# A residual block as nested fast convolution: row blocks, row sums and second-layer weights laid out anew, with a new order of all instructions

## The chip, the cores and the metric

The kernel runs on one core of one Trainium2 chip. The metric is the device time of one execution in microseconds (us). The kernel before took 462.77 us as the median of three runs (462.04 to 462.83).

## The reference

The input x has 2 images of 512 channels and 64 x 64 points in bf16. Group normalisation goes over 4 groups of 128 channels.

```python
def reference(x, t_emb, g1, be1, w1, w_emb, g2, be2, w2):
    ...
    def conv3(z, w):
        zp = jnp.pad(z, ((0, 0), (0, 0), (1, 1), (1, 1)))
        taps = [jnp.einsum("bchw,oc->bohw", zp[:, :, i:i+H, j:j+W], w[:, :, i, j]) for i in range(3) for j in range(3)]
        ...
    h = conv3(_silu(gn(x, g1, be1)), w1)
    emb = _silu(t_emb) @ w_emb
    h = h + emb.reshape(B, C, 1, 1)
    h = conv3(_silu(gn(h, g2, be2)), w2)
    return x + h
```

Two 3 x 3 convolutions from 512 to 512 channels carry nearly all the work.

## The kernel before

**Fast convolution.** The rows of an image are taken in groups of four (row r belongs to kind r modulo 4). From four kinds of rows and two halo rows, the kernel makes six *row planes* by sums, differences and scalings (`vplane`, s = 0 to 5). Each plane is multiplied by its own combination of the three weight rows, and the six results are combined into four output rows again. That saves matrix products and costs elementwise work. In most of the kernel the planes 0 to 3 are transformed once more along the columns (the "A" and "B" groups of matmuls with 256 columns), and in the last chunk the two outer planes 4 and 5 too (the "C" and "D" groups).

**Chunks and units.** A chunk `c` is a layer, an image and half of the rows: eight chunks, 0 to 3 for the first convolution and 4 to 7 for the second. A chunk has four input-channel tiles `ct` of 128 channels and four output-channel tiles `k`. The *unit* `u{c}{k}` makes one output tile: it runs the matmuls of TensorE (PE) into PSUM, the copies out of PSUM on ScalarE (ACT; `evac_o`, `evac_m`, `evac_pair`, `evac_b`), and VectorE's (DVE's) sums: "A", "s" and "d" on the four row results M, scalings by 8, 2 and 4, and "y" for the four output rows. `OO` holds the two outer results, which are added to two of the output rows ("O" on DVE, or "oa", an accumulating DMA of GpSimd's queue).

**Row blocks.** For each chunk and input tile, `load_a` brings the rows of a half image into a buffer of 18 strips (one strip, RP = 130 elements, is a row of a kind; four strips are a kind, PL = 520; `FO` orders the kinds). Before, the two halo strips are the first and the last one. `silu` works on it in place. `rows_a` and `rows_b` then make the planes: `k` is 4 times the block, then instructions of two kinds at a time, each written `two(base, r0, r1)`: two pieces of 520 elements, r1 − r0 apart. In the variant `early`, which only chunk 0 uses, the planes 4 and 5 are complete at the end of `rows_a`; otherwise their second term is added at the end of `rows_b` (by DVE, or with `vacc` by an accumulating DMA).

**Weights.** First-layer weights are combined on the core (`prep_w1`, `nest_w1`). Second-layer weights are combined by `prep_w2(j, ct)`, one output tile and one input tile at a time: two loads, two scalings on ACT, sums on DVE, one store to `u_scr` in HBM; two raw buffers are used in turn. `fetch_w2(j)` reads four of them back and adds the column combinations for the first chunk of layer 2; `stream_w2` takes later ones from HBM.

**Output.** The first layer's result goes to `h_scr` in HBM with its sums for the second normalisation. In layer 2 the output tensor is filled with x first (copies "pre" from HBM to HBM), and units accumulate into it by DMA; the last unit adds x on DVE.

**One tile, one order.** All buffers are slices of one large SBUF tile, `ar`. The semaphore waits between instructions are derived by the framework from the accesses to that tile, and it compares the block from an access's first to its last element. Each instruction is an operation of the class `Plan` with a number. `Plan.op` collects its predecessors element by element, and `emit` issues all operations, some 2,790, in the order of a long string `ORDER`, two characters per operation. Each engine executes its own in that order; SyncE's (SP's) queue issues the plain DMAs, GpSimd's (POOL's) the accumulating ones. `after` and `seq` are extra predecessors given by hand: `after` keeps a prefill copy behind the start of a unit four units earlier, `seq` keeps the first loads in sequence.

**Lines.** Small helpers record operations, so many instructions share a line: `tt` (L345, a DVE instruction with two tensor inputs), `ts` (L349, a DVE scaling), `act` (L368), `dma` (L383), `memz` (L387) and `mm` (L398). L1119 is the batch statistics of x's first tile.

Of the kernel before, what the change touches and what calls it, by code (L numbers as in the profile page):

```python
# [26 lines left out]
class Plan:  # L27
# [19 lines left out]
    def op(self, eng, cost, fn, r=(), w=(), name="", chain=False, lat=None, slack=0.0, after=None, sw=False, seq=None):  # L47
# [68 lines left out]
def _idx(off, dims):  # L116
# [6 lines left out]
FO = (3, 1, 2, 0)  # L123
# [3 lines left out]
AF = 18 * RP  # L127
VP = 4160
# [25 lines left out]
    'w2d': ((0, 0, 0, 0), (0, 0, 0, 0), (3, 3, 3, 3), (4, 0, 0, 0), (0, 0, 0, 0), (0, 0, 0, 0), (0, 0, 0, 0), (0, 0, 0, 0)),  # L154
# [14 lines left out]
    "0N002g0P0O0M0l010Q020304050607080k0R1G0j1D0a0i1E0g0p0b0h1F0m0o0n0c0q1I1H1J0r0s0d0t1K0u1L0T1M2Z1N0v0w240U0x0y2W0e0f1O130V"  # L169
    "1Y1i3P1P0X1Q1R1j0z1k160S210_1l3X1m2B0-1S2C1b0W1n2p090A0B0C0D0E0F2E0G0H0I0J0K0L1o102D1p1T111q2F2G1r4v191s3R2H1U122h2I1t2J"  # L170
    "1u142K1V2L1v1w3S151A0Z171C182M3Q1W1x2N1X1y1Z1z2O2P4Z1B1a1-1c2s1d4h3U1_2Q20272S223Y3Z2R2328252T261e2r2c2U2v2V3T2X1f2d2A2Y"
    "0Y2a2j2b1g2k292y2l1h2z3u2i2m2e2-2o4c2u2q2_2f303o2n313l4b323a333b3v2t4a343w3c353d364i4j2x37383e2w393f3C3A3g3n3x3r3B3y463D"
    "3h5e3F473i4k3E484e3W5W4m494l4A3V3j4B4d3G4C4n4D3H3z3K4o4G3q3-3I4H3J6b3k4I3m4p4J3p4K5Y4g4w4z4L3L4M5Z5f5g4N3s3M53434q3_5440"
    "4t4P555X4r564f3t574_584E6T504O594F5A4u4y6p5D5h5E4s6c6d5F5j416q5G425H5a6r5I5k5J8A5K6V5l5i5s4-445n4x5t8B5u4Q6U5v8C5x5m5y4R"
    "4U515zBS4SBT5-523N4T5_5b4V6061455p4W5o625L6W9F5M655C6e665B5q67BU5N3O685r6A6g6B5O5R5c6C6f5P6h6D5QBW6E696iBi9G6F5w7y6j6Y6G"
    "5S6H6s4X6k5T6X6t6l6u919H6v6oBV6n6x646y6zBaBXBk6-6_BY637071AK726I77Bj6mBb6J786ZBZ5d6aAL4Y79AM5U7ABP7C6K7D7B7E7F6L6O7G7H7I"
    "BmBc7J7N6MBQBe6N7ODR6w6P7PDZBl7gBdBo7Q6Q737h74Bn7R7iBRDa7K7SBp7j765V7kBg7TBf7U7lBh7m7n8D7o7L7p7q8E7rDS7V7s758F7t7W7u7MDc"
    "8G7vDb7w7X8IDT8J8K7xDd7z7-8L8MDV8NE_8ODf8PDh8U7Y8VDe7Z7_8W7aDO7b8X818Q8Z808Y8a8b8c9293828d8e8fDPA68g838k7c8l8R858m6R7d8H"
    "848nDj8S8o8i868s8pDQDU948q8hDX8r959I8tDW969JA7A8DiDY879K979L8TBB9N886S9O9P9Q9R989S8j9TDg9U9Z897f8u9aF0999bDl9c9AF79e8v9f"
    "9g9h9D8x9i9j9k8w9l9E9p8y9B9qF18z9M9r9V9sDkF38-9WA99tFFF29Y7e9uBCBDDn9vDmAA9wABAN9nF89CAO9dAC9mAP9XDA9xADAQ9o9yASAFATARAU"  # L180
# [12 lines left out]
    "LqMbJUMcJTMgMhL3MiMjLwMoMGNnMeMpMfLxMqL-KkLyMrNVMdKlMtLzMuL4MvMwMUMxNWMyMlMzQOQPMJMkM-L_N1KmN2N3N4N7NZN8MsMnN9M_NXNAN0Mm"
    "NqN5NaNrNBPQL5PCPDNsN6NbNtOkNYNvNwNCNxNyPENzM0N-N_O0OlL6O2NDO3NGOnPFO4NEPGRsNFNiO5L7M2O7O8NHQdO9OAOBOCODPHM1OENuOIOJNIOK"
    "PIOLOMMKO1ONQeOOOPPJNKOROoMLOSOTOUPKOVOWOXMMOYPTO6OpOmMNOFPUOqPOPVOQOGPWOHOZPYPLPZPaQQQRPbOaOrPcPdPeOsPfMOPhObQSPiMPPjRq"
    "OcPkNcOdRbRcPmRaQTPnOfPoPpNdOePqPrPXPsPNPtNJPxPgPyPzP-QUP_PuQ0Q1RrOgQ2Q4PlQ5Q6Q7QVQ8OhQ9QAT4PvQBQWQhPwOiQCQiPMUHQ3QjNlNe"
    "QkQYRdReQmQDSnQnOjQoQpQqQrQXQsQtQvQENfQwQIQFQxQaQGQyQZQHQ-T2Q_QuR0QcR1R2QbR3RfR4R5R9SoSpRAUGRBNgRCRDREQJRFQlRGRIQzRtRJRK"
    "RhQLRHRLRMRNRgRORPR6QKRiRuT3NhRvRjR7RQRwRkRxWhSqSrRlRzQMR-R8R_S0S1RmT1S2S3S4RpSsS6RnS7T_U0RoS8UES9SuSBSCStSDWgSESvSFSGSH"
    "RRSISwSMSNS5VCVDSOUFSPSySQSRRySSRSSTSVT-SWSxRWSXSYSZRTSaSbScS_RVVBT5RUT6SASzT7SJXuRXT8TAT0SURYTBTCOtTDOuTESdOvSKTFTGTHOw"
    "SLTJOxTKSeTITLOySfTMRZOzSgSjTOVSTPTQO-TRShO_TSP0TTP1SiTUP2S-TVTZVTTWTaP3TbP4TcP5P7TdP6T9TeP8SkTfU1U2TgTiVRTjTkTlTYSlTmTn"  # L200
    "ToTXTpUIThUJTqUKU3ULTrUNUOUPTsUQURTNUSU5UTSmUUUWUVU6UXU4U7UYTtWOVEVFUZU8U9UbUcVUUdTwUeUAUfTuUgUhUBTvWPWQUiUmUnVGUCUoUpUq"
    "UrUsUDUtWeUvUwUMTxUxUyUjUzU-WfU_VIV0TyVVUuVHVWV1VJVXUlXbVKVYUkUaVaVMWRWSVbVcVdVLVeVfTzVgV2XcXdVhVjVkVNVlV3XrWTVQVmV4VoVp"
    "VqVPVrV5YpWUYqVsVtViVuVvV7VzWVV-VwV_W0W1W2V6W3WWW4W6VnW7V8YoW8WXW9WAVZWBWCVOV9WDW5WiaOVyWjWEWYWkWZXeXfWlVxXtWnWaWoWpWqWF"
    "WrWsXgWtWuWwWcWxWGYrYsWya3Xha4beXiWzWHXsW_X0X1WvX2X3WbZ5X4VAX5X6WJWKXAXjXBWIXCaNXDWdX7XEXFXGWLa2XHXJXkXKXLWmXMXmWMXNW-XO"
# [14 lines left out]
def kernel(  # L219
# [39 lines left out]
    RAW = [Z + 2176, Z + 4096]  # L259
# [249 lines left out]

    def um1(j, ct, kx, pos):  # L510
        return A(um_off(j) + ct * 2048 + kx * 512 + pos * 128, [[1, 128]])

    def st_off(s, ct):
        return um_off(2 * s + ct // 2) + 8192 + (ct % 2) * 768

    rawc = [0]

    def row_w(w0, w2z, mid, o_um, name, TB):

        p = A(TB, [[384, 2], [1, 384]])  # L520
        if abs(w2z[1] - w2z[0]) < 32768:
            tt(p, A(w0, [[0, 2], [1, 384]], BF16), A(w2z[0], [[w2z[1] - w2z[0], 2], [1, 384]], BF16), ALU.add, name)
        else:
            for i in range(2):
                tt(A(TB + i * 384, [[1, 384]]), A(w0, [[1, 384]], BF16), A(w2z[i], [[1, 384]], BF16), ALU.add, name)
# [5 lines left out]
    def wsrc(w, j):  # L531

        return w[j]
# [853 lines left out]
```

## Time and profile before

| | |
|---|---|
| median of three runs | 462.77 us |
| profiled execution, its own time | 460.75 us |
| its span | 458.8 us |
| TensorE busy | 442.3 us, 2904 matmuls |
| VectorE busy | 435.3 us, 811 instructions |
| ScalarE busy | 407.0 us, 611 instructions |
| GpSimd busy | 59.6 us |
| DMA | 93.82 MB, mean 204 GB/s |
| granted TensorE clock | 0.997 |

A profile records one execution. "Busy" is the time in which an engine executes something. DVE instructions that follow each other without a wait overlap a little, so the distance from start to start is shorter than the busy time of one. A row of a timeline gives start, length, engine, line, operation, operands and how many instructions it joins; "idle before, <-releaser" tells what ended the engine's idle time. A row of groups ends with busy time and mean of one, then idle time before. The chain of waits is followed back from the last instruction. In windows cut by time, the columns after the window are its length and the busy times of PE, PEld (weight load), DVE, ACT and POOL with their instructions, then the clock, the DMA share and GB/s.

### The profile page before, as it was taken

The page shows a single profiled execution, that of the slowest core. Times are in us where ns is not written, and L with a number is a line of the kernel's source. Part 1 is how long each engine was busy: PE and PEld are TensorE (multiplying, and loading weights), DVE is VectorE, ACT ScalarE, POOL GpSimd, SP SyncE. Part 2 cuts the span into 40 slices and gives each one's busy share as a digit, 9 for nine tenths or more (in the row PEclk, how much of TensorE's full clock was granted, in tenths as well). Part 3 has the DMA queues.
Part 4 walks back from the last instruction along what each step waited for, and adds up shares of the span by engine and source line. Part 5 has one row for each costly group of instructions (what it writes and reads, how often), then busy time and mean ns, then how long its engine had stood idle before and what let it go on. Part 6 is the DMA issues. An engine that isn't in the chain of part 4 may idle for free. (4 is left out here: it accounts for less than half of the span.)

```text
span 458.8 us, 8186 instructions
## 1 busy us (share of the span) xinstructions
PE 442.3 (96%) x2904; PEld 281.7 (61%) x2904; DVE 435.3 (95%) x811; ACT 407.0 (89%) x611; POOL 59.6 (13%) x94
## 2 busy tenths in 40 slices
PE   8999999999999899999999979999999999999995
PEld 4644444455555556656666556666666666788882
DVE  2899999999999999999999999999899999999995
ACT  5799999999989999999999999878999969757662
POOL 1110010111111101111000001212221223111220
PEclk9999999999999999999999999999999999999998
DMA  8963452587666468576877957898796999776754
GB/s 323 401 242 95 173 181 58 144 274 211 171 184 202 134 192 235 155 247 203 290 230 229 338 184 224 186 269 213 172 239 158 281 244 240 178 186 124 175 97 93
DMA packets 45480, 93.82 MB, mean 204 GB/s; under 512 B 8704, under 2 KB 20352, under 8 KB 45440
## 3 DMA queue, kind: packets, MB, share of 16 engines
q1 hardware_dynamic: 34512, 78.92, 51.2%
q0 software_dynamic: 10640, 14.38, 20.3%
q8 instruction: 22, 0.36, 0.3%
q14 instruction: 18, 0.15, 0.1%
q10 hardware_dynamic: 288, 0.01, 0.0%
HBM read 63.57 MB, written 31.32 MB: 207 GB/s over the span
## 5 line engine op out<-in xcount | busy, mean ns | idle before, releaser
L398 PE MATMUL psum<-ar 128*128 128x256 f16 (+2 forms) x2771 | 421.6, 313 | 8.3 <-ACT ar L368 4.6
L345 DVE TENSOR_TENSOR ar<-ar 128x1024 f16<-128x1024 f16 (+7 forms) x630 | 411.0, 711 | 9.5 <-ACT ar L368 6.0
L398 PEld LDWEIGHTS <-ar 128*128 128x128 f16 (+1 forms) x2763 | 267.9, 98 | 158.7 <-issue 14.4
L368 ACT ACTIVATE ar<-ar 128x512 f16<-128x512 f16 (+6 forms) x186 | 189.3, 1058 | 22.8 <-DVE ar L345 21.3
L368 ACT ACTIVATE ar<-psum 128x512 f16<-128x512 f32 (+3 forms) x250 | 159.8, 694 | 16.1 <-PE psum L398 8.9
L368 ACT ACTIVATE ar<-ar,fs 128x2304 f16<-128x2304 bf16 (+1 forms) x32 | 74.1, 2320 | 4.0 <-DVE fs L491 3.4
L383 POOL DMA_DIRECT2D ar<-ar x26 | 30.2, 1184 | 116.1 <-DVE ar L345 100.0
L387 POOL MEMSET ar<- 128x65 f16 (+3 forms) x41 | 6.8, 177 | 206.5 <-ACT ar L368 196.8
L383 POOL DMA_DIRECT2D out_dram<-ar x15 | 18.7, 1244 | 47.6 <-DMA ar<-ar 31.0
L368 ACT ACTIVATION_READ_ACCUMULATOR ar<-psum 128x1 f32 x104 | 24.8, 239 | 0.0
L349 DVE TENSOR_SCALAR ar<-ar 128x520 f16<-128x520 f16 (+3 forms) x50 | 19.7, 405 | 0.5 <-POOL ar L387 0.5
L398 PEld LDWEIGHTS <-ones_bf 128*128 128x128 bf16 x88 | 8.8, 105 | 6.9 <-issue 2.7
L398 PE MATMUL psum<-ones_bf 128*128 128x512 bf16 x32 | 9.2, 454 | 1.1 <-DVE ones_bf L402 1.1
L368 ACT ACTIVATION_READ_ACCUMULATOR ar<-ar 128x1 f32 x36 | 7.6, 211 | 0.0
L398 PE MATMUL psum<-ar,ones_bf 128*128 128x260 bf16 x56 | 7.1, 274 | 0.0
L398 PEld LDWEIGHTS psum<-fs,ones_neg 128*128 128x128 f32 x36 | 4.6, 191 | 3.1 <-ACT ar L368 1.7
L1119 DVE BATCH_NORM_STATS2 fs<-ar 128x6 f32<-128x512 bf16 x4 | 2.5, 682 | 4.1 <-DMA ar<-in_x_dram 4.1
L398 PE MATMUL psum<-fs,ones_neg 128*128 128x1 f32 (+3 forms) x36 | 4.6, 246 | 1.7 <-DVE fs L1124 1.0
L476 POOL TENSOR_TENSOR fs<-fs 128x1 f32<-128x1 f32 x4 | 3.3, 832 | 15.4 <-DVE fs L474 15.3
L436 ACT ACTIVATE s_sb<-tparm 128x18 bf16<-128x18 bf16 x1 | 0.2, 218 | 2.9 <-DMA tparm<-in_t_emb_dram 2.9
L430 ACT ACT_TABLE_LOAD x1 | 1.3, 1283 | 1.7 <-PEq L1371 1.7
L398 PE MATMUL psum<-ar,s_sb 128*2 128x512 bf16 x9 | 2.7, 377 | 0.0
(54 smaller groups left out, 23.3 us busy)
## 6 DMA issues: line engine op xcount, KB each, us to landing
ar<-in_w_dram SPq DMA_DIRECT2D x36, 384.0 KB, 5.0
ar<-in_x_dram SPq DMA_DIRECT2D x16, 585.0 KB, 4.7
h_scr<-ar SPq DMA_DIRECT2D x16, 520.0 KB, 5.1
ar<-h_scr SPq DMA_DIRECT2D x16, 520.0 KB, 4.8
out_dram<-in_x_dram SPq DMA_DIRECT2D x30, 260.0 KB, 6.0
out_dram<-ar POOLq DMA_DIRECT2D x15, 520.0 KB, 7.3
ar<-in_x_dram SPq DMA_DIRECT2D x13, 520.0 KB, 5.2
u_scr<-ar SPq DMA_DIRECT2D x16, 384.0 KB, 3.8
```

The lines of the kernel that those rows point to most:

```text
L345: pl.op("DVE", 0.075 + 0.000521 * out.n, lambda: nc.vector.tensor_tensor(out=out.ap, in0=a.ap, in1=b.ap, op=op), regs(a, b), regs(out), name)
L349: pl.op("DVE", cost or 0.075 + 0.00026 * out.n, lambda: nc.vector.tensor_scalar(out=out.ap, in0=a.ap, scalar1=s, scalar2=None, op0=ALU.mul ...
L368: lambda: nc.scalar.activation(out=out.ap, in_=a.ap, func=func, scale=sc, **kw), regs(*rr), regs(*ww), name)
L383: lambda: eng.dma_start(out=out, in_=in_, **kw), regs(*r), regs(*w), name, lat=3.2 if sw else None, after=after, sw=sw, seq=seq)
L387: pl.op("POOL" if eng == "gpsimd" else "DVE", 0.08 + 0.0005 * out.n, lambda: e.memset(out.ap, v), (), regs(out), name)
L398: nc.tensor.matmul(out.ap, lhsT=lhsT.ap, rhs=rhs.ap, start=st, stop=sp, skip_group_check=True)
L430: nc.scalar.activation(out=fs[:, WARM:WARM + 1], in_=fs[:, WARM + 1:WARM + 2], func=ACT.Silu)
L436: nc.scalar.activation(out=s_sb[:], in_=tparm[:], func=ACT.Silu)
L476: pl.op("POOL", 0.85, lambda: nc.gpsimd.tensor_tensor(out=F(rs, n).ap, in0=N.ap, in1=F(NEGH, n).ap, op=ALU.pow), regs(N), regs(F(rs, n)), ...
L1119: pl.op("DVE", 0.61, lambda: nc.vector.bn_stats(out=q.ap, in_=e.ap), regs(e), regs(q), nm)
```

## The change

- **Row blocks.** The halo strips move from the ends of the block (strips 0 and 17) to the end of each half (strips 8 and 17), and the kinds stand in the order 1, 2, 3, 0. Loads of x and h without halo become two pieces of 1040 elements per partition. `rows_a` and `rows_b` always use the variant that was `early`; `vacc` is gone. The number of DVE instructions per tile stays.
- **Row results and sums.** The four results M lie in slots (1, 3, 2, 0), so that pairs and sums lie apart from each other; the "A" sum of four is one flat access. The outer results `OO` are contiguous and the output rows that they go to are neighbours; "oa" is one flat DMA.
- **Second-layer weights.** `prep_w2` makes a pair of input tiles: 8 calls instead of 16, with one raw buffer instead of two, three DVE instructions and two stores each. `fetch_w2` has three instructions of 2048 elements instead of six of 1024. The host lays w2 out for this, and `um1` and `st_w` index it.
- **Order.** `after` and `seq` are no predecessors any more. `ORDER` is new as a whole. The matmul groups keep their order except at the start; loads, prefill copies, DVE and ACT operations move.
- In counts: DVE operations built 806 before and 770 after, ACT 475 and 459, SP's DMAs 231 and 215, matmuls and their weight loads 5744 and 5750 (the Gram matrices of the first statistics have one more product each).

The diff, cut to its core:

```diff
-        if after is not None:
-            deps.add(after)
         o.seq = seq
-        if seq is not None:
-            deps.add(seq)
...
-FO = (3, 1, 2, 0)
+FO = (1, 2, 3, 0)
+HF = AF // 2
...
-    'w2d': ((0, 0, 0, 0), (0, 0, 0, 0), (3, 3, 3, 3), (4, 0, 0, 0), ...
+    'w2d': ((0, 0, 0, 0), (0, 0, 0, 0), (2, 1, 2, 1), (2, 0, 0, 0), ...
...
-    def prep_w2(j, ct, eng="ACT"):
-        ...
-        k = rawc[0] % 2
-        rb, ob = RAW[k], W2O[k]
-        ...
+    def prep_w2(j, h):
+        nm = f"w2_{j}{2 * h + 1}"
+        flat = A(RAW, [[1, 1536]], BF16)
+        dma(flat.ap, w2[j][:, h * 1536:(h + 1) * 1536], [], [flat], P * 3072, nm)
+        m = A(RAW + 2304, [[1, 768]], BF16)
+        dma(m.ap, w2[j][:, 3072 + h * 768:3072 + (h + 1) * 768], [], [m], P * 1536, nm)
+        scal("ACT", A(RAW + 1536, [[1, 768]], BF16), A(RAW + 768, [[1, 768]], BF16), 4.0, nm)
+        scal("ACT", A(RAW + 3072, [[1, 768]], BF16), m, 2.0, nm)
+        p = A(WS, [[1, 1536]])
+        tt(p, A(RAW, [[0, 2], [1, 768]], BF16), A(RAW + 768, [[1, 1536]], BF16), AD, nm)
+        cut = lambda o, dt=None: A(o, [[768, 2], [256, 3], [1, 256]], dt)
+        for i, op in ((1, AD), (0, SB_)):
+            tt(A(W2O[i], [[256, 2], [512, 3], [1, 256]]), cut(WS), cut(RAW + 2304, BF16), op, nm)
+        for i in (1, 0):
+            ov = A(W2O[i], [[1, 1536]])
+            dma(u_scr[j][:, 2 * h + i], ov.ap, [ov], [K("u", j, 2 * h + i)], P * 3072, nm)
...
     def fetch_w2(j):
...
-        for c in range(0, CT, 2):
-            g = lambda kx: A(um_off(j) + c * 2048 + kx * 512, [[2048, 2], [1, 512]])
+        g = lambda kx: A(um_off(j) + kx * 512, [[2048, 4], [1, 512]])
+        t = A(WB[0], [[512, 4], [1, 512]])
...
+    G1, G2, D0, G3, G0, D5, H0 = 0, PL, 2 * PL, 2 * PL + RP, 3 * PL + RP, 3 * PL + 2 * RP, AF - RP
...
-    G3, G1, G2, G0, D5 = RP, RP + PL, RP + 2 * PL, RP + 3 * PL, 2 * RP + 3 * PL
...
-    def rows_a(c, ct, w, keng, early):
+    def rows_a(c, ct, w, keng):
...
         tt(two(w, G1, G2), two(ab, G3, D5), two(w, G1, G2), SB_, nm)
-        if early:
-            tt(two(w, 0, G0), two(w, 0, G0), two(ab, G1, G2), SB_, nm)
-            tt(v45, two(w, 0, G0), two(w, G1, G2), AD, nm)
-        else:
-            tt(v45, two(w, 0, G0), two(ab, G1, G2), SB_, nm)
+        tt(two(w, D0, G0), two(w, D0, G0), two(ab, G1, G2), SB_, nm)
+        tt(A(s4, [[s5 - s4, 2], [1, PL]]), two(w, D0, G0), two(w, G1, G2), AD, nm)
...
-        rb = G2 if early else G0
-        tt(two(w, 0, rb), two(ab, G3, G0), two(ab, G1, G2), SB_, nm)
+        tt(two(w, D0, G2), two(ab, G3, G0), two(ab, G1, G2), SB_, nm)
...
+        slot = (1, 3, 2, 0)
+        M = lambda i: A(MB + slot[i] * 512, [[1, 512]])
+        MM = lambda i, j: A(MB + slot[i] * 512, [[(slot[j] - slot[i]) * 512, 2], [1, 512]])
...
-            tt(M(0, 4), M(0, 4), A(SD, [[512, 4], [1, 512]]), AD, nm + "A")
+            tt(A(MB, [[1, 2048]]), A(MB, [[1, 2048]]), A(SD, [[1, 2048]]), AD, nm + "A")
-        tw = lambda off, st: A(off, [[st, 2], [1, 512]])
-        tt(tw(SD, 1024), M(0, 2), M(2, 2), AD, nm + "s")
-        tt(M(0, 2), M(2, 2), M(0, 2), SB_, nm + "d")
+        tt(A(SD + 512, [[512, 2], [1, 512]]), MM(0, 1), MM(2, 3), AD, nm + "s")
+        tt(MM(0, 1), MM(2, 3), MM(0, 1), SB_, nm + "d")
...
-        yo = A(ys, [[3 * PL, 2], [1, PL]])
-        oo = A(OO[1], [[OO[0] - OO[1], 2], [1, PL]])
+        yo = A(ys + 2 * PL, [[1, 2 * PL]])
+        oo = A(OO[1], [[1, 2 * PL]])
```

More of the change, by code (lines that the diff above doesn't have):

```diff
@@ L120, in _idx @@
     return idx
-FO = (3, 1, 2, 0)
+SB_, AD = ALU.subtract, ALU.add
+FO = (1, 2, 3, 0)
 RP = 130
@@ L258 @@
     WX = Z
-    RAW = [Z + 2176, Z + 4096]
+    RAW = Z + 2176
     W2O = [Z + 6016, TB]
@@ L510, in um1, with st_w @@
     def um1(j, ct, kx, pos):
[L511 to L522, printed above, removed]
-        else:
-            for i in range(2):
-                tt(A(TB + i * 384, [[1, 384]]), A(w0, [[1, 384]], BF16), A(w2z[i], [[1, 384]], BF16), ALU.add, name)
-        m = A(mid[0], [[mid[1] - mid[0], 2], [128, 3], [1, 128]], BF16)
-        p3 = A(TB, [[384, 2], [128, 3], [1, 128]])
-        tt(A(o_um + 256, [[128, 2], [512, 3], [1, 128]]), p3, m, ALU.add, name)
-        tt(A(o_um, [[128, 2], [512, 3], [1, 128]]), p3, m, ALU.subtract, name)
-    def wsrc(w, j):
-        return w[j]
+        return A(um_off(j) + (ct // 2) * 4096 + (pos // 2) * 2048 + kx * 512 + (pos % 2) * 256 + (ct % 2) * 128, [[1, 128]])
+    def st_w(s, ct, ky, kx):
+        return A(um_off(2 * s + ct // 2) + 8192 + ky * 768 + kx * 256 + (ct % 2) * 128, [[1, 128]], BF16)
     def load_ur(j, seq=None):
@@ L598, in fetch_w2 @@
         dma(d.ap, u_scr[j], [K("u", j, c) for c in range(CT)], [d], P * 4 * 3072, nm)
[L599 to L604 removed]
+        g = lambda kx: A(um_off(j) + kx * 512, [[2048, 4], [1, 512]])
+        t = A(WB[0], [[512, 4], [1, 512]])
+        tt(t, g(0), g(2), AD, nm)
+        tt(g(3), t, g(1), AD, nm)
+        tt(g(1), t, g(1), SB_, nm)
     def stream_w2(s, j):
@@ L713, in rows_b @@
             tt(A(o[k], [[o[k + 1] - o[k], 2], [1, PL]]), Q, SS, op, nm)
-        if not early:
-            v45 = A(s4, [[s5 - s4, 2], [1, PL]])
-            t0 = two(w, G1, G2)
-            if vacc:
-                d, t = A(s4, [[1, 2 * PL]]), A(w + G1, [[1, 2 * PL]])
-                dma(d.ap, t.ap, [t, d], [d], P * 4 * PL, f"va{c}{ct}", sw=True, acc=True)
-            else:
-                tt(v45, v45, t0, AD, nm)
         if md == "N":
@@ L847, in evac_pair @@
         def evac_pair(s, bank):
-            act(M(s, 2, 1024), Ps(bank, 0, [[512, 2], [1, 512]]), ACT.Copy, scale=KAP[s], name=nm + f"m{s}")
+            act(MM(s, s + 2), Ps(bank, 0, [[512, 2], [1, 512]]), ACT.Copy, scale=KAP[s], name=nm + f"m{s}")
         def evac_b(s, bank):
@@ L854, in evac_b @@
             else:
-                act(A(BT + s * 512, [[1024, 2], [1, 512]]), Ps(bank, 0, [[512, 2], [1, 512]]), ACT.Copy,
+                act(A(BT + slot[s] * 512, [[(slot[s + 2] - slot[s]) * 512, 2], [1, 512]]), Ps(bank, 0, [[512, 2], [1, 512]]), ACT.Copy,
                     scale=0.5 * KAP[s], name=nm + "b")
@@ L910, in unit @@
             run([(b1, 1, B_mms)])
-            act(A(BT + 512, [[1, 256]]), Ps(b1, 0, [[1, 256]]), ACT.Identity, scale=0.5 * KAP[1], acc=acc(6), name=nm + "b")
-            act(A(BT + 768, [[1, 256]]), Ps(b1, 256, [[1, 256]]), ACT.Copy, scale=0.5 * KAP[1], name=nm + "b")
+            act(A(BT + 1024, [[1, 256]]), Ps(b1, 0, [[1, 256]]), ACT.Identity, scale=0.5 * KAP[1], acc=acc(6), name=nm + "b")
+            act(A(BT + 1280, [[1, 256]]), Ps(b1, 256, [[1, 256]]), ACT.Copy, scale=0.5 * KAP[1], name=nm + "b")
             s_ops()
@@ L1017, in unit @@
             seg = lambda base, r0, n, dt=None: A(base + r0 * PL, [[1, n * PL]], dt)
-            dma(seg(xa, 0, 4, BF16).ap, x[b, k, ch][:, RP:RP + YF], [], [seg(xa, 0, 4)], P * YF * 2, nm + "x")
-            tt(seg(ot, 1, 2, BF16), seg(ys, 1, 2), seg(xa, 1, 2, BF16), AD, nm + "x")
-            end = A(ys, [[3 * PL, 2], [1, PL]])
-            tt(end, end, A(xa, [[3 * PL, 2], [1, PL]], BF16), AD, nm + "x")
-            for r0, n, i in ((1, 2, None), (3, 1, 0), (0, 1, 1)):
+            dma(A(xa, [[2 * PL, 2], [1, 2 * PL]], BF16).ap, xmain(b, k, ch), [], [seg(xa, 0, 4)], P * YF * 2, nm + "x")
+            tt(seg(ot, 0, 2, BF16), seg(ys, 0, 2), seg(xa, 0, 2, BF16), AD, nm + "x")
+            end = seg(ys, 2, 2)
+            tt(end, end, seg(xa, 2, 2, BF16), AD, nm + "x")
+            for r0, n, i in ((0, 2, None), (3, 1, 0), (2, 1, 1)):
                 if i is not None:
@@ L1145, in stats0, with ones @@
         b_ = psum[:]
-        def ones(base, first, slow):
-            mm([(Ps(bk, 0, [[1, 260]]), cone, A(base + i * 260, [[1, 260]], BF16), first and i == 0, False)
+        def ones(base, first, slow, gap=0):
+            mm([(Ps(bk, 0, [[1, 260]]), cone, A(base + i * 260 + gap * (i // 4), [[1, 260]], BF16), first and i == 0, False)
                 for i in range(8)], nm, chain=False, slack=0.0, slow=slow)
@@ L1152, in gram @@
             lst = []
-            for i in range(17):
-                n = 128 if i < 16 else 32
-                blk = A(base + i * 128, [[1, n]], BF16)
+            for i in range(18):
+                n = 128 if i % 9 < 8 else 16
+                blk = A(base + (i // 9) * HF + (i % 9) * 128, [[1, n]], BF16)
                 q_ = psum[0:n]
                 lst.append((R(bass.AP(q_.tensor, q_.offset + bk * 512 + G0, [list(q_.ap[0]), [1, n]]),
-                              ("P", np.array([bk])), n), blk, blk, False, i == 16))
+                              ("P", np.array([bk])), n), blk, blk, False, i == 17))
             mm(lst, nm, chain=False, slack=0.0, slow=slow)
@@ L1164, in stats0 @@
             for i in range(4):
-                bn_stats(A(XB0[ct] + RP + i * PL, [[RP, 4], [66, 2], [1, 64]], BF16), F(bst + 6 * i, 6), nm)
+                bn_stats(A(XB0[ct] + RP * (i // 2) + i * PL, [[RP, 4], [66, 2], [1, 64]], BF16), F(bst + 6 * i, 6), nm)
         else:
-            ones(XB0[ct] + RP, True, cold[0])
+            ones(XB0[ct], True, cold[0], RP)
             if CFG["st0"][ct] == "A":
-                act(junk(), A(XB0[ct] + RP, [[1, YF]], BF16), ACT.Square, scale=(sc / HW) ** 0.5, acc=F(mg), name=nm)
+                act(junk(), A(XB0[ct], [[HF, 2], [1, 2 * PL]], BF16), ACT.Square, scale=(sc / HW) ** 0.5, acc=F(mg), name=nm)
             else:
-                gram(XB0[ct] + RP, cold[1])
+                gram(XB0[ct], cold[1])
         ones(XB1[ct], half, 1.0 if half else cold[2])
@@ L1210 @@
         silu(0, ct)
-        rows_a(0, ct, WB[ct % 3], CFG["k0"][ct], True)
+        rows_a(0, ct, WB[ct % 3], CFG["k0"][ct])
         for j in range(3):
@@ L1216 @@
             mm(plain_mms(2 * j + 1, 0, j, ct, 5), "o")
-        rows_b(0, ct, WB[ct % 3], CFG["t0"], True)
+        rows_b(0, ct, WB[ct % 3], CFG["t0"])
     prs[0] = 2
@@ L1252, in prod @@
         w = WB[0] if l == 0 else WS
-        rows_a(c, ct, w, CFG["k"][c], False)
-        rows_b(c, ct, w, CFG["t"][c], False, ct < CFG["vacc"][c])
+        rows_a(c, ct, w, CFG["k"][c])
+        rows_b(c, ct, w, CFG["t"][c])
         if c == 7 and CFG["no"]:
@@ L1283 @@
             for i in range(CFG["w2d"][c][k]):
-                prep_w2(w2n[0] // 4, w2n[0] % 4)
+                prep_w2(w2n[0] // 2, w2n[0] % 2)
                 w2n[0] += 1
@@ L1294 @@
                     r0, r1 = i * YF // 2, (i + 1) * YF // 2
-                    dma(out[b, k, ch][:, r0:r1], x[b, k, ch][:, RP + r0:RP + r1], [], [K("o", b, k, ch, i)],
+                    dma(out[b, k, ch][:, r0:r1], x[b, k, ch][:, i * HF:i * HF + 2 * PL], [], [K("o", b, k, ch, i)],
                         P * YF * 1.4, f"pre{c}{k}", after=ufirst[max(ucnt[0] - CFG["pre"], 0)])
@@ L1339, in wl, with wl2 @@
         w = w.reshape(4, 128, 4, 128, 3, 3).transpose(0, 3, 2, 4, 5, 1)
+        o = w[:, :, :, [0, 2]].reshape(4, 128, -1)
+        mid = w[:, :, :, 1].reshape(4, 128, -1)
+        return np.concatenate([o, mid], axis=2)
+    def wl2(w):
+        w = w.reshape(4, 128, 2, 2, 128, 3, 3).transpose(0, 4, 2, 5, 6, 3, 1)
         o = w[:, :, :, [0, 2]].reshape(4, 128, -1)
```

203 lines of the change are left out of this document (90 added, 113 removed).

## The prediction

> **What bounds the kernel now.** I read the page's busy shares first, then the windows cut by stage, then VectorE (DVE) by shape, then its timeline and the chain of waits, and last the waits of TensorE (PE).
>
> ```profile
> span 458.8 us, 8186 instructions
> ...
> PE 442.3 (96%) x2904; PEld 281.7 (61%) x2904; DVE 435.3 (95%) x811; ACT 407.0 (89%) x611; POOL 59.6 (13%) x94
> ```
>
> Three engines are nearly full, so the stages decide, not the mean:
>
> ```profile
> 40.00:140.00 100.00, 99.12 (x514) 49.41 (x513) 97.84 (x191) 97.76 (x166) 8.71 (x14) 1.00 0.59 173
> 140.00:240.00 100.00, 98.03 (x629) 61.19 (x627) 99.38 (x194) 99.28 (x196) 8.68 (x16) 1.00 0.68 210
> 240.00:340.00 100.00, 96.45 (x670) 65.20 (x668) 96.69 (x161) 91.66 (x119) 13.81 (x21) 1.00 0.82 232
> 340.00:417.00 77.00, 75.47 (x562) 54.67 (x561) 76.13 (x119) 63.72 (x69) 16.18 (x18) 1.00 0.85 206
> 417.00:448.00 31.00, 30.86 (x283) 27.48 (x282) 29.23 (x57) 20.70 (x28) 6.04 (x5) 1.00 0.68 135
> ```
>
> The columns are PE, PEld, DVE, ACT, POOL, clock, DMA share, GB/s. From 140 to 240 us DVE and ACT are both at 99%; from 340 DVE alone is (76.1 of 77). From 417 PE is dense to 448. The chain that ended last agrees:
>
> ```profile
> 398.88 1.30 DVE ar L345 x2
> ...
> 400.31 4.25 DVE ar L345 x6
> ...
> 417.13 2.89 PE psum L398 x25
> ...
> 420.05 28.12 PE psum L398 x256
> ...
> 452.91 0.69 DVE ar L345
> ...
> 453.63 0.71 DVE ar L345
> ```
>
> DVE (from 398) hands over to PE at 417, at the last row block's outer tiles. Whatever is gained before 417 moves everything behind it, if PE and ACT follow.
>
> Matmul starts lie 215.5 ns (512 columns) and 109 ns (256) apart in the trace. Those intervals sum to 432 us. At each PE group I take actual start minus this running sum, the *lag*: 8.8 us at 40.8 us, 14.6 at unit 20's A groups, 15.5 before unit 40, 18.5 after its A1, 23.5 at 420. Where a group starts within 0.6 us of the end of an input, that engine caused the growth. That gives about 7.5 us of growth to DVE (3.1 at chunk 1's first unit, 2.7 at chunk 2's, the rest late) and about 6 to ACT. PE's waits show the second part:
>
> ```profile
> PE psum L398 <- ACT ar L368: 5.3, 8, 2.8
> PE psum L398 <- DVE ar L345: 3.2, 5, 1.0
> ```
>
> The 2.8 is unit 40's A1, which waits for the ACT copy of its B pair.
>
> **Part 1: fewer DVE instructions.** The shapes:
>
> ```profile
> L345 DVE TENSOR_TENSOR ar<-ar 128x1024 f16<-128x1024 f16 x181 | 119.7, 683 | 0.6
> L345 DVE TENSOR_TENSOR ar<-ar 128x2048 f16<-128x2048 f16 x63 | 76.4, 1219 | 5.7 <-ACT ar L368 5.3
> L345 DVE TENSOR_TENSOR ar<-ar 128x768 f16<-128x768 f16 x64 | 34.2, 550 | 0.1
> L345 DVE TENSOR_TENSOR ar<-ar 128x1536 f16<-128x1536 f16 x32 | 30.0, 949 | 0.0
> 24.01 1.30 DVE L345 TENSOR_TENSOR ar<-ar 128x1040 f16<-128x1040 f16 x2
> ```
>
> Durations don't add: the two in the last row start 1.30 − 0.69 = 0.61 us apart though each is busy 0.69. Start to start, back to back, single rows of the trace give 336 ns (512 elements), 469 (768), 602 (1024), 869 (1536), 1136 (2048): 0.521 ns per element and about 68 fixed. The change keeps the elements and drops 36 instructions: 48 of 768 become 24 of 1536 (pairs in prep_w2), 24 of 1024 become 12 of 2048 (fetch_w2). 36 x 68 = 2.45 us.
>
> The Trainium skill (VectorE: DVE Perf Modes, The DRAIN you can't avoid) says that the next operation starts only when the pipe is empty, and "Minimize op *count*, not sems". The same page grants that an instruction which nothing holds starts earlier, and the row with two inside 1.30 us shows that; by the stricter rule the 36 would be worth their whole fixed 150 ns each, 5.4 us as an estimate.
>
> **Part 2: fewer waits of DVE on itself.** In the chain rows, instructions that read their predecessor's result start 453.63 − 452.91 = 0.72 us apart; single rows of the 1040 shape lie 727 ns apart then, against 611 without the wait: 116 ns. The dependences of one big tile go by covering blocks. Before, an instruction on halves 0 and 3 of the row block covers the halves between, so it waits for an instruction that shares no element with it. In the built program 82 DVE instructions wait for the one just ahead of them, afterwards 58. 40 of the former have no true overlap (23 between row steps, 11 and 5 between rows_b and rows_a, 1 other), afterwards none; the new order makes some true ones. 24 x 116 = 2.8 us. Waits on older DVE instructions fall too, but those are long finished: nothing.
>
> Parts 1 and 2: −5.25 us over the whole run. Summed in issue order up to the DVE instruction that each PE group needs, DVE time falls by 2.6 us at chunk 2, 2.7 at unit 50, 4.6 at unit 60, 5.1 at unit 70, and 4.0 to 5.5 at unit 70's outer tiles. At unit 10's A2 it rises by 1.5.
>
> **Part 3: ACT.** 32 scalings of 384 columns (413 ns start to start) become 16 of 768 (about 733): −1.5 us. Half of the 64 pair evictions become flat; the trace has only the split kind (1.02 us for 2 x 512, which is already less than two of 0.62), so a flat one is bounded by 20 ns either way, 0.6 us in all; I take nothing. With what the order moves, ACT's sum up to unit 40's B copy falls by 2.2 us.
>
> **Part 4: DMA.** x and h loads go in 2080-byte pieces instead of 4160 (85 ns a packet against 161): +2.1 us of 16 engines' time in all. The "oa" accumulations go from 1040- to 2080-byte packets (104.5 against 180): −5. w2 loads: −1. All spread under transfers that have cover; taken as nothing. If cover is missing, one x or h load lands later by 2.1/29, below 0.1 us.
>
> **Part 5: the start.** Before, silu of the first tile starts at 15.1 us; DVE's first statistics wait for x00:
>
> ```profile
> 8.95 2.47 DVE L1119 BATCH_NORM_STATS2 fs<-ar 128x6 f32<-128x512 bf16 x4 [4.06 <-DMA ar<-in_x_dram]
> ```
>
> x00 is issued third of the loads (x10 landed at 4.4, x11 5.9, x01 7.5, x00 8.9); afterwards it is behind x01 and x10 only, so about 7.7. silu moves to about 13.9. The first weights are now behind x12 and x02 (w1_0 at about 20 instead of 11.8), just where the first scaled row is due (20.5); three prefill copies of the output enter SP's queue in the first 30 us, ahead of loads that are due there. I take −1.2 us, bounds −1.5 and +1 (w1_0 late by one load: x01 and x00 landed 1.4 us apart, of which the earlier silu gives some back).
>
> **Part 6: a new wait.** The first fetch of second-layer weights (1.5 MB, 7.9 us from issue to landing) now has its first DVE use at a running sum of 210.6 us, before 214.2. About 2.2 us of slack goes. 0 to +2; I take +0.5, since DVE is then about 4 us earlier but has other rows issued ahead. Behind that instruction DVE's next row block queues, and PE's chunk 4 behind that.
>
> **The sum.** Not DVE's 5.25 but what PE can follow. Up to unit 40: start −1.2, ACT −2.2 at the A1 gate, −3.4 together (DVE allows about as much: −2.6 − 1.2). After that PE lags by another 5 us: 3.1 of it is the loop between PE and ACT (a bank is emptied and refilled), which nothing here shortens; the 1.3 that DVE causes (units 50, 60 and 70) goes, and 0.6 that I can assign to neither stays. New wait +0.5. So −3.4 − 1.3 + 0.5 = −4.2. The last unit has as many DVE instructions after PE's end as before: nothing. The profiled execution took 460.75 us (span 458.8 and 1.95 around it), 0.4% under the median 462.77: 460.75 − 4.2 = 456.55 there, 458.6 as the median. What a measurement can tell from no change is about 0.2%, 0.9 us.
>
> **Rivals.** *All of DVE's gain arrives:* PE's loop waits shrink with it, since ACT's in-order queue (u40b) is itself held by DVE at 27.4 us of "ACT <- DVE". Then −5.25 − 1.2 + 0.5: 456.8. For: the chain from 398 to 417 is DVE alone. Against: PE groups after unit 50 that start 0.05 us behind an ACT copy.
>
> *Waits on itself cost nothing,* because DVE catches up while PE or ACT holds it: part 2 gone. −2.45 − 1.2 + 0.5 = −3.15: 459.6. For: DVE idles only 7 us from 40 to 447, so little catching up is possible; this speaks mostly against. The Trainium skill's section above has this as its rule (a semaphore after each instruction measured no longer than one at the end); 727 against 611 contradicts it.
>
> *Nothing left:* the start is +1 instead of −1.2 and the fetch costs 2: −4.2 + 2.2 + 1.5 = −0.5: 462.3.
>
> *Slower:* prep_w2 has one RAW buffer instead of two. A pair's load stands in SP's in-order queue until the pair before it has been scaled and summed; x and h loads, h stores and prefill copies stand behind it, then silu, rows and PE. There are 7 hand-overs; a 384 KB load takes 5.0 us to land. If each exposes 1 us: +7 − 4.2 = +2.8, 465.6. It decides from 0.6 us each. For: DMA share 0.68 to 0.82 then, and DVE has no slack. Against: a pair has twice the work of a tile, so there are half as many hand-overs.
>
> **Chances.** My sum 0.40, all of DVE's gain 0.22, waits free 0.17, nothing left 0.07 (half of it within 0.2%), slower 0.14. Range: low end all of DVE's gain with its bounds (no new wait −0.5, start −0.3, ACT −1.5): 454.5. High end takes in "nothing left" with 1 us of room: 463.3. Left out: slower, and some beyond the low end. Faster 0.82, same 0.04, slower 0.14.
>
> **What would show it.** Right: DVE about 775 instructions, busy down by about 36 x 150 = 5.4 us (waits are not busy), about 24 fewer 0.73 us intervals; 1040 rows still at 694; first silu near 14; the chain's hand-over to PE near 413; PE waiting for ACT 4 to 5 us still. Wrong: DVE idle before the 2048 rows with DMA as releaser (the fetch), SP-fed loads landing late before silu in chunks 2 and 3 (the buffer), or PE waiting in the first 40 us on weights.

## The result

The changed kernel takes 455.57 us (median of six runs, 455.22 to 457.85) against 462.26 of the kernel before in the same comparison; ratio 0.9873, 95% interval 0.9843 to 0.9902. In three later groups of runs it came to 0.9890, 0.9882 and 0.9909. The profiled execution took 456.01 us against 460.75: −4.74, where −4.2 was forecast. The median moved by 6.7, which goes with the granted clock: in the three later groups 40 of 48 executions of the kernel before had less than 0.996 and took 461.0 to 463.5 us (the other eight 460.3 to 460.9), most of the changed kernel had 0.996 or more, and at 0.996 or more the medians lie 3.9 to 4.7 us apart in each group.

The page of the changed kernel, then its windows (PE, PEld, DVE, ACT, POOL, clock, DMA share, GB/s):

```profile
span 454.1 us, 8086 instructions
...
PE 441.3 (97%) x2907; PEld 282.1 (62%) x2907; DVE 430.3 (95%) x775; ACT 406.0 (89%) x595; POOL 52.7 (12%) x94
```

```profile
40.00:140.00 100.00, 100.00 (x521) 50.06 (x520) 98.80 (x186) 98.21 (x160) 6.76 (x15) 1.00 0.63 189
140.00:240.00 100.00, 99.44 (x638) 62.19 (x637) 98.77 (x176) 99.03 (x189) 6.82 (x16) 1.00 0.78 247
240.00:340.00 100.00, 97.62 (x693) 67.59 (x692) 95.98 (x155) 93.19 (x119) 13.73 (x21) 1.00 0.73 196
340.00:417.00 77.00, 75.20 (x566) 55.02 (x564) 75.45 (x121) 61.46 (x68) 14.51 (x18) 1.00 0.74 174
417.00:448.00 31.00, 31.00 (x263) 25.44 (x261) 28.46 (x54) 19.11 (x26) 4.79 (x4) 1.00 0.69 147
```

TensorE is now busy without a gap from 40 to 140 us (99.12 before) and at 99.4 up to 240 (98.03); that is where most of the time came from. From 340 its share is no better than before, and DVE still has work in all but 1.5 of the 77 us. The groups of DVE and TensorE's two waits:

```profile
L342 DVE TENSOR_TENSOR ar<-ar 128x1040 f16<-128x1040 f16 x197 | 132.4, 697 | 1.0 <-ACT ar L365 0.4
L342 DVE TENSOR_TENSOR ar<-ar 128x1024 f16<-128x1024 f16 x157 | 104.9, 688 | 3.1 <-ACT ar L365 2.1 <-issue 0.5
L342 DVE TENSOR_TENSOR ar<-ar 128x2048 f16<-128x2048 f16 x75 | 90.9, 1222 | 4.9 <-ACT ar L365 3.7 <-DMA ar<-u_scr 0.9
L342 DVE TENSOR_TENSOR ar<-ar 128x1536 f16<-128x1536 f16 x48 | 45.4, 960 | 0.0
```

```profile
PE psum L395 <- ACT ar L365: 3.7, 5, 1.7
PE psum L395 <- DVE ar L342: 2.0, 4, 0.7
```

775 instructions instead of 811. TensorE's waits fell from 5.3 and 3.2 us. The chain's hand-over from DVE to TensorE moved from 417.1 to 413.87:

```profile
411.59 2.23 DVE ar L342 x4
413.87 29.23 PE psum L395 x266
```

TensorE's lag (start of a group minus the sum of the matmul intervals ahead of it), worked out as in the prediction, shows where the time came off. A1 or B2 is a group's kind and its row plane. All numbers in us:

| group | before | after | difference |
|---|---|---|---|
| unit 00 | 8.78 | 8.59 | −0.19 |
| unit 10, B2 | 11.88 | 10.52 | −1.36 |
| unit 20, B0 | 14.57 | 10.86 | −3.71 |
| unit 30, A0 | 15.42 | 11.92 | −3.50 |
| unit 40, A0 | 15.49 | 12.97 | −2.52 |
| unit 40, A1 | 18.45 | 14.80 | −3.65 |
| unit 53, first group | 20.83 | 15.48 | −5.35 |
| unit 60, A1 | 21.71 | 16.69 | −5.03 |
| unit 71 | 23.50 | 18.24 | −5.26 |

### The profile page after: what moved, and what is told of

Same layout as the page of the kernel before. It is cut to its first block, busy times and chain, and to the rows that moved or that the text cites. A ratio compares the mean times of both kernels' runs of the same rounds, so it can differ in the third digit from the quotient of the medians.

```text
span 454.1 us, 8086 instructions
## 1 busy us (share of the span) xinstructions
PE 441.3 (97%) x2907; PEld 282.1 (62%) x2907; DVE 430.3 (95%) x775; ACT 406.0 (89%) x595; POOL 52.7 (12%) x94
## 4 chain that ended last, share of the span: by engine, by line
DVE 19%; ACT 18%; PE 6%; issue 5%; DMA 5%; SPq 0%; DVEq 0%; ACTq 0%
DVE ar L342 18%; ACT ar L365 18%; PE psum L395 6%; DMA ar<-h_scr 4%; DMA out_dram<-in_x_dram 1%; SPq L380 0%; DVE ar L346 0%; DVEq L1352 0%; DVEq L342 0%; DVE fs L482 0%; DVE fs L483 0%; DVE fs L1029 0%; DVE fs L1040 0%; DVE fs L1033 0%; DVE fs L479 0%
## 5 line engine op out<-in xcount | busy, mean ns | idle before, releaser
L395 PE MATMUL psum<-ar 128*128 128x256 f16 (+3 forms) x2774 | 420.5, 313 | 5.5 <-ACT ar L365 3.4
L342 DVE TENSOR_TENSOR ar<-ar 128x1040 f16<-128x1040 f16 (+5 forms) x594 | 406.5, 750 | 10.0 <-ACT ar L365 7.1
L395 PEld LDWEIGHTS <-ar 128*128 128x128 f16 (+2 forms) x2766 | 268.1, 98 | 154.7 <-issue 9.0
L365 ACT ACTIVATE ar<-ar 128x512 f16<-128x512 f16 (+6 forms) x170 | 187.4, 1136 | 18.5 <-DVE ar L342 15.3
L365 ACT ACTIVATE ar<-psum 128x512 f16<-128x512 f32 (+4 forms) x250 | 160.8, 689 | 17.5 <-PE psum L395 11.2
L380 POOL DMA_DIRECT2D ar<-ar x26 | 23.2, 920 | 135.2 <-DVE ar L342 95.8
L384 POOL MEMSET ar<- 128x65 f16 (+3 forms) x41 | 9.5, 259 | 187.7 <-ACT ar L365 187.7
L395 PE MATMUL psum<-ones_bf 128*128 128x512 bf16 x32 | 11.4, 467 | 1.1 <-DVE ones_bf L399 1.1
L473 POOL TENSOR_TENSOR fs<-fs 128x1 f32<-128x1 f32 x4 | 3.5, 863 | 15.7 <-DVE fs L471 15.4
```

Of the source, the lines that this page charges most:

```text
L342: pl.op("DVE", 0.075 + 0.000521 * out.n, lambda: nc.vector.tensor_tensor(out=out.ap, in0=a.ap, in1=b.ap, op=op), regs(a, b), regs(out), name)
L365: lambda: nc.scalar.activation(out=out.ap, in_=a.ap, func=func, scale=sc, **kw), regs(*rr), regs(*ww), name)
L380: lambda: eng.dma_start(out=out, in_=in_, **kw), regs(*r), regs(*w), name, lat=3.2 if sw else None, after=after, sw=sw, seq=seq)
L384: pl.op("POOL" if eng == "gpsimd" else "DVE", 0.08 + 0.0005 * out.n, lambda: e.memset(out.ap, v), (), regs(out), name)
L395: nc.tensor.matmul(out.ap, lhsT=lhsT.ap, rhs=rhs.ap, start=st, stop=sp, skip_group_check=True)
L473: pl.op("POOL", 0.85, lambda: nc.gpsimd.tensor_tensor(out=F(rs, n).ap, in0=N.ap, in1=F(NEGH, n).ap, op=ALU.pow), regs(N), regs(F(rs, n)), ...
```

## The experiments

Theory 1: the gain comes from DVE, which has 36 instructions less and waits less often for its own last instruction. Rival A: such waits cost nothing. Rival B: the gain is the new order as such. The runs came in three groups; each has the kernel before beside it, and the changed kernel as a base.

**Base of the first group.** The changed kernel, unedited.

> The changed kernel itself, as the common base of this group. Both theories: 455.6 us, as before within 0.2%.

Measured 456.67 us, ratio 0.9890 (0.9871 to 0.9910).

**Own waits put back.** An instruction of the row steps gets a dependence on the DVE instruction ahead of it, where both are row steps and share no element:

```diff
...
+            if last is not None and ins is not None and last[0].i not in o.preds and o.name[:3] in ("row", "rob") and last[0].name[:3] in ("row", "rob"):
+                self.tc.add_manual_dep(ins.ins, last[1].ins.name, mybir.DependencyInfo(
+                    mybir.DependencyClass.Sync, mybir.DependencyReason.DATA), reason="as before")
...
```

> The changed kernel, where 111 VectorE instructions of the row steps wait in addition for the VectorE instruction just ahead of them, though they share no element with it; 169 such waits instead of 58. Theory 1: 111 x 116 = 12.9 us more VectorE time, 9 to 13 of it at the end: 464.6 to 468.6 us. Rival A (waits on the last instruction cost nothing): 455.6 within 0.2%.

Measured 467.45 us, ratio 1.0135 (1.0112 to 1.0159): +10.8 us against the base, 97 ns for each wait. Rival A is out. TensorE's wait for DVE shows it (us in total, times, longest), against 2.0 in 4 of the changed kernel:

```profile
PE psum L407 <- DVE ar L354: 8.7, 11, 1.7
```

In the trace, 48 DVE instructions of the changed kernel start 10 to 60 ns after the end of the one ahead; here 144. What these cost beyond the back-to-back distance rises from 5.3 to 16.8 us, 120 ns each. So nearly all of DVE's time (10.8 of 11.5) reaches the end. The Trainium skill (VectorE: DVE Perf Modes, The DRAIN you can't avoid) reports that a semaphore after each operation cost nothing extra in a chain of copies. This run disagrees for a queue in which instructions otherwise overlap.

**Instructions given back.**

```diff
-        tt(p, A(RAW, [[0, 2], [1, 768]], BF16), A(RAW + 768, [[1, 1536]], BF16), AD, nm)
+        tt2([A(WS + q * 768, [[1, 768]]) for q in range(2)], [A(RAW, [[1, 768]], BF16)] * 2,
+            [A(RAW + 768 + q * 768, [[1, 768]], BF16) for q in range(2)], AD, nm)
...
```

The other two sums of a pair and the three of `fetch_w2` are cut likewise.

> The changed kernel with the 36 VectorE instructions given back: each of the 24 of 1536 elements in the second-layer weight pairs and the 12 of 2048 in the fetches is issued as two halves, one behind the other. Theory 1: 36 x 68 ns = 2.45 us more VectorE time, 1.0 to 2.5 of it at the end: 456.6 to 458.1 us. By the stricter rule (an instruction starts only when the last has finished) 36 x 150 = 5.4: up to 461.0. Rival B (order alone): 455.6 within 0.2%.

Measured 457.98 us, ratio 0.9933 (0.9908 to 0.9957): +1.3 us. The back-to-back distances sum to 425.3 us instead of 422.9, 67 ns for each of the 36 (68 forecast), and TensorE's lag at unit 71 rises from 18.7 to 20.7. Not 150 ns each, as by the stricter rule. Of the 2.4 us, about half reaches the end (1.3).

**Own waits hidden by order alone, in the kernel before.** The edit is in the order string only: 31 DVE instructions move forward by one to four places.

> The kernel before with 31 VectorE instructions moved forward by one to four places, so that they stand between an instruction and the one that waits for it; waits on the instruction just ahead fall from 82 to 56, nothing else changes. Theory 1 (a wait of VectorE on its own last instruction costs 116 ns and VectorE sets the pace): 26 x 116 = 3.0 us less of VectorE time, of which PE follows at least half: 459.3 to 460.8 us. Rival A (such waits cost nothing at the end): no change, 462.3 within 0.2%. Rival B (the new order as such brings the gain, by when each transfer and copy comes): no change either, since no transfer, copy or matmul moves.

Measured 462.85 us, ratio 1.0026 (1.0011 to 1.0041): not a gain but 1.2 us lost. Theory 1 missed here. The cost of own waits did fall, from 7.6 to 5.8 us, but DVE's waits for ACT rose, where the kernel before had 6.0 in 9:

```profile
DVE ar L345 <- ACT ar L368: 9.3, 15, 2.9
```

I read this so: an instruction put in between saves 0.12 us and holds back the one that others need by its own 0.6. TensorE's lag at unit 10's B2 went from 11.88 to 13.00, but 0.76 of that stood at unit 00 already. Later it exceeds the lag of the kernel before by 0.3 us at unit 20, 1.1 at unit 30, 0.6 at unit 40's A1 and 2.0 at unit 51, so the loss comes at several places. No run takes the 31 moves apart. By this reading a shorter DVE queue is a gain only if what is urgent doesn't move back. The change's new placement takes the false waits away without moving anything in between.

**All three counts given back, in the new order.** The split above, 32 scalings on ACT instead of 16, and 24 own waits (82, as before).

> The changed kernel in its own new order, with the three counts of the kernel before given back: the 36 VectorE instructions split again, the 16 weight scalings on ScalarE split into 32, and 24 waits of row steps on the VectorE instruction just ahead (82 such waits instead of 58). Theory 1 (counts and waits of VectorE make the gain): +1.3 (measured for the split) + 24 x 0.097 = 2.3 (from 10.8 us for 111 waits) + up to 1.5 for ScalarE: 460 to 461.5 us, within 0.4% of the kernel before. Rival B (the new order as such makes the gain): 456 to 458 us.

The base of this group:

> The changed kernel itself, as the common base of this group. All theories: a ratio of 0.988 to the kernel before, about 456.3 us.

The base measured 455.80 us, ratio 0.9882 (0.9857 to 0.9906). Against it the kernel with the counts of before took 460.14, ratio 0.9968 (0.9954 to 0.9982): 4.3 of the group's 5.8 us come back with the counts. Most of the other 1.5 us goes with the clock: all nine executions with the counts of before had 0.997 to 0.999, and the two of the kernel before at 0.996 or more in this group took 460.45 and 460.55. Against those about 0.4 us is left for the new order together with the flat accesses and fuller packets (1.1 between the two profiled executions); these were not separated.

**ACT's scalings split, alone.**

```diff
-        scal("ACT", A(RAW + 1536, [[1, 768]], BF16), A(RAW + 768, [[1, 768]], BF16), 4.0, nm)
+        scal2(h2(RAW + 1536), h2(RAW + 768), 4.0, nm)
...
```

> The changed kernel with the 16 ScalarE weight scalings of 768 columns split into 32 of 384. Theory 1 with ScalarE as a second bound (unit 40 waits for its B copy behind them): 16 x 0.093 = 1.5 us more ScalarE time before unit 40, 0.5 to 1.5 at the end. Rival: ScalarE has slack, no change within 0.2%.

Measured 456.53 us, ratio 0.9883 (0.9863 to 0.9903), against 0.9882 of the base: nothing. The lag at unit 40's A1 is 14.83; in the changed kernel it was 14.56 to 14.80 in the first three profiles. ACT's count is not in the gain.

**The start.** One sum of the first weights moves behind the row steps of the fourth tile (order string only).

> The changed kernel with one VectorE instruction of the first weights (0.96 us, ahead of the third tile's row steps at 28.4 us) moved behind the fourth tile's row steps. If TensorE's lag at unit 00 is set by the third and fourth row steps (the start's forecast gain of 1.2 us came to 0.2 there): unit 00 starts 0.5 to 0.9 us earlier, and 0.3 to 0.9 of it is left at the end. Rival: the lag is taken up again at unit 30 or 40, where VectorE or ScalarE is the last to be ready, and the end is unchanged within 0.2%.

Measured 455.21 us, ratio 0.9859 (0.9840 to 0.9878), within the spread of the base. In the DVE timelines, first of the changed kernel, then of this one, the fourth tile's scaling (0.73 us, second of its shape) starts 0.8 us earlier:

```profile
28.42 0.95 DVE L342 TENSOR_TENSOR ar<-ar 128x1536 f16<-128x1536 f16 x1
...
32.74 0.73 DVE L346 TENSOR_SCALAR ar<-ar 128x2210 f16<-128x2210 f16 x1
```

```profile
28.63 0.73 DVE L346 TENSOR_SCALAR ar<-ar 128x2210 f16<-128x2210 f16 x1
...
31.92 0.73 DVE L346 TENSOR_SCALAR ar<-ar 128x2210 f16<-128x2210 f16 x1
```

Unit 00's lag falls to 7.79 (8.59 to 9.12 in the changed kernel's profiles). At unit 30 0.1 to 1.1 is left against the changed kernel's four profiles, at unit 40's A1 nothing (14.61, against the 14.56 to 14.80 above). The rival holds in the trace: something at unit 40 takes the start's gain up.

**What unit 40 waits for.** In the changed kernel ACT works on a sum of squares up to 264.5 us and then does unit 40's B copy. I moved that sum behind the copies.

> The changed kernel with one ScalarE instruction (the 1.9 us sum of squares of unit 32, at 262.6 us) moved behind the two copies of unit 40's B pairs. If unit 40's A1 groups wait for ScalarE's queue order: TensorE's lag there falls from 14.7 to 12.9 or 13.3 (the B groups' own lag is 12.9), and 0.5 to 1.5 us is left at the end: ratio 0.985 to 0.987. Rival: the second normalisation's sums (unit 41's groups wait for them 0.5 us later) or VectorE at unit 60 take it up, no change within 0.2%.

The base of this group:

> The changed kernel itself, as the common base of this group: ratio 0.988 to the kernel before.

The base measured 457.49 us, ratio 0.9909 (0.9890 to 0.9928); the kernel with the sum moved 459.13, ratio 0.9947 (0.9927 to 0.9968): slower. ACT's timeline with the sum out of the way:

```profile
260.28 1.98 ACT L365 ACTIVATE ar<-ar 128x512 f16<-128x512 f16 x3
264.13 2.43 ACT L365 ACTIVATE ar<-psum 128x1024 f16<-128x1024 f32 x3 [1.87 <-DVE ar L342]
```

ACT stands idle for 1.87 us, and DVE releases it. The instruction is DVE's "O" sum of unit 33 (the row gives its duration three times, in ns, and its start):

```profile
L342 DVE TENSOR_TENSOR ar<-ar x1: 693/693/693, 263.3 to 263.3; 128x1040 f16<-128x1040 f16 x1
...
who waited for it (us, times):
  ACT ar L365: 1.9, 1
```

It ends at 264.04 and reads the outer results at Z + 9088 (`O0`), where unit 40's B copy writes (`BT1`, from Z + 8704). It ended at 264.38 in the changed kernel and at 267.88 before, and the copy began 0.1 us after it both times. ACT was at work up to that moment too in those (to 264.51 and 268.00), so there both engines come ready together; only this run takes them apart. With ACT out of the way the lag at unit 40's A1 is 14.5, against 14.6 to 15.4 in the changed kernel's four profiles and the 12.9 or 13.3 expected: the gate that the profile books under ACT is held by DVE as well. Meanwhile the second normalisation's sums come later by the sum of squares, and unit 41's lag rises from 15.3 to 16.9. TensorE now waits for ACT ahead of the small products of that normalisation, where it did not wait in the changed kernel:

```profile
272.90 0.61 PE L395 MATMUL psum<-fs,ones_neg 128*128 128x8 f32 x4 [1.88 <-ACT ar L365]
```

That is the place that the rival named, though it expected no change at the end.

**Both moves.** The order has the move in the start and the move at unit 40.

> The move at unit 40 together with the move in the start (lag at unit 30 was 11.8 instead of 12.5 with it, and 14.6 as ever at unit 40's A1). If unit 40 was what took up the start's gain: lag there 12.2 to 12.8, and 1.0 to 2.0 us less at the end than the changed kernel: ratio 0.984 to 0.986. Rival: no more than one of the two alone, ratio 0.986 to 0.988.

Measured 458.30 us (456.96 to 462.2), ratio 0.9933 (0.9913 to 0.9953): neither expectation, no better than the changed kernel. Its lags can't be compared as they stand, since the first statistics began at 9.64 us there (x00 late), and at 7.75 to 8.66 in the changed kernel's. Their growth can: 1.8 us at unit 40's A1, as in the changed kernel, and then the wait of the last run again, so that with this move nothing could be left of the start's gain:

```profile
274.79 0.93 PE L395 MATMUL psum<-fs,ones_neg 128*128 128x8 f32 x4 [1.89 <-ACT ar L365]
```

**The placement alone, in the old order.** The changed kernel with `prep_w2`, `fetch_w2` and the host layout of before; operations take the places that those of the same name had.

> The new placement of row blocks, row results and sums alone, with the old second-layer weights and the old order, in which the sum of the planes 4 and 5 now stands right behind the difference that it reads. VectorE has as many instructions as before, and 108 instead of 82 wait for the one just ahead (the false ones are gone, true ones are added). Theory 1: 26 x 0.097 = +2.5 us against the kernel before, ratio 1.005. Rival C (the placement helps by itself, by flat accesses and larger packets): ratio 1.000 or less.

Measured 476.04 us, ratio 1.0304 (1.0276 to 1.0332): a miss for both. Own waits explain 2.9 us (10.55 instead of 7.64), a late start another 2.1. But TensorE's waits for ACT rose from 5.3 as well:

```profile
PE psum L396 <- ACT ar L366: 13.1, 15, 3.8
DVE ar L343 <- ACT ar L366: 11.2, 19, 2.3
```

In the variant of `rows_a` that is now used everywhere, one more sum stands ahead of the steps of `rows_b`; I take it that an order made for the other variant keeps DVE late throughout, but no run takes that apart. The run doesn't price the placement; it shows that this placement isn't worth having with that order.

## Why the prediction was right or wrong

**The forecast.** The profiled execution came within 0.6 us of it (456.01 against 456.55). The median came 3.0 us under it (455.57 against 458.6): I had subtracted from a median of 462.77, a time that the kernel before later showed only at a granted clock below 0.996. As the steps below show, the size of the sum is partly luck.

**Parts 1 and 2 hold.** DVE's back-to-back distances fell from 425.7 to 422.9 us (−2.8; 2.45 forecast) and what own waits add from 7.6 to 5.3 (−2.3; 2.8 forecast). 74 instructions started just behind the end of the last one before, 48 do now, 26 fewer; 24 were forecast. About 20 of the 26 were released by DVE itself; they carry the 2.3 us. Put back, they cost 1.3 us (the split), 10.8 (111 waits) and 4.3 (all counts together) at the end.

**The start failed as a step.** −1.2 was forecast, −0.19 came at unit 00, and in the three later profiles of the changed kernel the lag there is 8.9 to 9.1, above the 8.78 of before. (x00 was the fourth load before, not the third as I wrote; the statistics that wait for it began at 8.11 us, with 7.7 forecast for its landing.) silu did start at 14.12 instead of 15.1, and the first two tiles' row steps ended 3 us earlier. But I took that for the whole stage. What ends last is the third and fourth tile, whose planes 4 and 5 were ready at 32.82 and 36.84, against 32.35 and 36.64 before: the new order has three of the first weights' sums on DVE between 25.4 and 29.4. Nor would the gain have lasted, as the move in the start shows.

**The gate at unit 40: size right, cause only in part.** I added ACT's −2.2 to the start's −1.2 and got −3.4; −3.65 was measured. But splitting ACT's work back changed nothing, and with ACT out of the way DVE still held the copy. DVE's sum of unit 33 came 3.50 us earlier. Summed over the two traces up to it, 0.9 of this is the sum of the back-to-back distances, 0.9 own waits and 1.7 idle time of DVE that is gone, 1.5 of it in the first 105 us. So the terms that count are near those that the prediction has only in brackets, as what DVE allows (−2.6 − 1.2); that ACT's term and the start's gave the same size is luck. In the sum the wait is put down to the engine that the row names; that this engine is itself held by DVE stands in the prediction only under its first rival. That DVE alone set the gate before the change isn't shown, since ACT came ready at the same moment.

**After unit 40** 1.3 was forecast and 1.6 came (5.26 − 3.65). TensorE's and ACT's loop did not stay as it was: units 43, 51 and 53 no longer wait (1.6 of lag before), while units 60 and 61 wait more (1.9 against 0.9). Which unit waits varies with the execution: in the profiles of the second and third base, unit 53 has 1.0 and 1.4 us again.

**The new wait** came in another place and small: DVE waited 0.9 us for the second fetch (the row of 2048 above), and no group of TensorE began right behind it. **The end** gave back a little: TensorE's last group came 5.07 earlier, the span 4.7.

**The rivals.** "All of DVE's gain arrives" (456.8) names the mechanism better than my sum does, but not its share: in the reverse direction 10.8 of 11.5 us arrived for the waits and 1.3 of 2.4 for the split, and of the 5.1 us that DVE saved (2.8 + 2.3) 3.9 to 4.7 arrived at a granted clock of 0.996 or more. The forecast of 4.2 lies within that. "Waits cost nothing" is refuted. "Slower" by the single raw buffer: no sign; where the pairs are made TensorE's share rose (windows up to 240 us).

## What to carry to other kernels

Where several buffers share one tile, place what is read and written in turn so that the blocks from first to last element don't meet: the same instructions then overlap, wherever the order doesn't set two side by side of which one truly needs the other (the new placement in the old order had 108 own waits instead of 82). Hiding such a wait behind other work is worth its tenth of a microsecond only if the work that moves back is not urgent. And follow a wait one step further than the row that names it: the engine named may itself be waiting for the one that has been tuned.

## What the runs showed of the hardware

The first loads land at different times in executions of the same start: the statistics that wait for x00 began at 7.75 to 8.66 us in four profiles of the changed kernel, and at 9.64 in the variant with both moves, which issues the same loads in the same order. The time goes with the granted clock: the kernel before took 460.27 to 460.92 us at 0.996 or more, 460.95 to 462.19 at 0.993 or 0.994, and 462.21 to 463.45 at 0.990. And a wait on the instruction just ahead is not absorbed by a nearly full VectorE: 111 of them added 11.5 us to its queue and 10.8 us to the kernel.
